# Sparse attention with a gated FFN on one core: batch 0 takes its near keys from the turned keys and its V products in column halves, ScalarE joins in scaling P, and the order of the instructions is new

## The chip, the core and the metric

The kernel runs on one core of a Trainium2 chip. A core has TensorE (PE, matrix products, with its weight loads listed as PEld), VectorE (DVE), ScalarE (ACT), GpSimd (POOL) and SyncE (SP, which issues DMAs). Each engine works through its own list in order; semaphores hold an instruction until its inputs are there and its output's place is free. The metric is the device time of one execution in microseconds (us), as the median of several runs.

## What is computed

Block-sparse attention of 4 batches, 8 heads, 768 rows and head size 64, and behind it a gated feed-forward network (FFN). A row may look at its own and the two neighbouring blocks of 32 rows, at the first and the last block, and at three sampled blocks per block of queries; the first and the last block of queries look at all keys.

```python
scores = q @ k.T / sqrt(64)              # per batch and head
mask = near | first or last block (query or key) | sampled blocks
attn = softmax(where(mask, scores, -1e9))
x = (attn @ v)                           # to (3072, 512)
out = (sigmoid(x @ w_gate) * (x @ w_val)) @ w_out   # d_ff = 1536
```

## The kernel before

A small planner class holds some 1,400 operations (`P(name, engine or engines, estimated duration, function, ...)`). The durations take no part when the kernel is built: `Planner.run` (L207) reads the table `ORDER` (L51 to L172) and issues the operations in that order. An item is `name:engine` and the numbers of the buffers or banks that it takes; engines are P, A (ACT), D (DVE), G (POOL) and S (SP). `+n` on a PE item puts n filler matmuls of 128x512 on zeros ahead of it (L1064), so PE is never idle long.

Each batch goes through these operations (batch number first, then the block or step):

- `ldk`, `ldq`, `ldv` (L415) load and cast to f16, issued by POOL. For batches 1 to 3 `rrk`, `rrq` put rows in order on POOL (L529). `trk`, `trq` turn K and Q on PE (L549 in batch 0, L545 later), `evk`, `evq` bring them from PSUM to the tiles KT and QT (L565 to L569) on ACT or DVE.
- `vsh` copies V by rows (L578, on DVE), `scr` writes it to a scratch tensor in DRAM (L586, L590, by SP). From there `w` (L662, SP) loads windows of near V rows into V1, and `vg` (L729, SP, three DMAs a block) the sampled V rows into V2. `vfl` (L627) fills the rows of the first and last block into V1 and V2, on POOL, or DVE in batch 0. `regSP` and `regPOOL` load the sampled block numbers into registers.
- Keys: each of 11 steps takes two blocks of queries. `kfl` puts the first and last key block in a tile KG, `kg` gathers the sampled ones there (L698, POOL), and `kw` copies the near keys there too (L712, on POOL or DVE). `sc` is then 16 score matmuls of 256 columns (L768) and 8 or 16 mask matmuls (L757), all on quarter-width tiles of the array (two row halves, four column quarters).
- `mx` takes the row maximum (L780, DVE), `ex` the exponential with the row sum, in two halves (L790, ACT), `rz` the reciprocal (L799, DVE), and `sl` scales P by it: one instruction of 512 elements on POOL (L808) or two of 256 on DVE (L811). `tp` turns P on PE (L823), `te` copies it out of PSUM as PTS (L829, ACT or DVE).
- `pv` is the product with V (L841): per step 16 matmuls with 128 columns of V as weights and 64 columns moving, of which only half of each result is wanted. `xe` copies the wanted halves to XT, one instruction per half of the partitions (L868, L870), on ACT or DVE.
- The first and last block of queries are dense: `dsc` (16 matmuls of 384 columns, L897), `dmx` (L908), `dex` (L914), `dsl` (L923), `dtp` (L931), `dte` (L940), `dpv` (32 matmuls, L951), `dxe` (L975, L977). In batch 0 the keys lie in KT with 8 neighbours together, and `dsc` reads every eighth, so that it writes PSUM without gaps.

The FFN takes the rows in nine groups of 128 to 512. For each of 12 slices, `pg` and `pu` are four matmuls each (L1010), `th` a tanh on ACT (L1019), `h` the product on DVE (L1024); then `py` is 12 matmuls for each 128 rows (L1041), `ys` scales (L1048 DVE, L1050 ACT) and `st` stores (L1055). The weights come in nine loads `wg`, `wv`, `wo` of three parts each (L429, L437), issued by POOL. Groups 0 and 1 hold 128 rows each of batch 0; group 2 has 256 rows and begins when batch 0's attention is nearly done. From there on the FFN of one batch runs between the attention steps of the next.

PSUM has eight banks: scores take pairs of 0, 1, 2 (and 5, 6 for batch 0's first steps), P and V products 3 and 4, the FFN 5, 6 and 7. Three options matter here. `merge` 'm' is the scheme with near keys in KG; '.' puts masks first and takes near keys (96 columns) straight from KT and the others (160) from KG, in two matmuls. `tiled` 'u' is the V product above; 't' takes only the wanted half: weights of 64 columns, 32 columns moving, twice as many matmuls, and one copy instruction instead of two. `sl` names the engines that may scale P.

## Time and profile before

| | |
|---|---|
| median of 3 runs | 338.52 us (337.54 to 338.83) |
| the profiled execution | 338.99 us |
| its span | 337.1 us |
| instructions | 11706 |
| matmuls that are fillers | 113 |
| DMA packets, bytes | 43001, 42.09 MB |
| mean of all DMA queues | 125 GB/s |
| granted PE clock | full in every slice of the span |

The span runs from the first to the last instruction of the profiled execution. In what follows, rows of the profile give the engine, the line of the kernel, the operation, output <- input by the names of the tiles, the partitions and elements and the count. Rows by shape end in busy time in us, the mean of one in ns, and the idle time of the engine ahead of them with what ended it. Timelines and the chain of work that ended last begin with start and length in us. Matmuls overlap, so the cost of one in a row of many is the distance of the starts.

### The profile page before, as it was taken

What the parts mean: (1) busy time and instruction counts of PE and PEld (TensorE: products, weight loads), DVE (VectorE), ACT (ScalarE), POOL (GpSimd) and SP (SyncE); (2) the same over time, 40 slices, a digit from 0 to 9 for tenths busy, and PEclk for the clock granted to TensorE, in tenths of its full rate; (3) what the DMA queues carried; (4) which work ended last, traced back from release to release, by engine and by line L of the source; (5) the groups of instructions that cost most, each with busy time, mean ns of one, the idle gap of its engine ahead of it and who ended that gap; (6) DMA issues with size and microseconds to landing.
All of it is one profiled execution on the core that took longest, in us unless ns stands there. A gap on an engine that the chain in (4) does not pass through costs nothing.

```text
span 337.1 us, 11706 instructions
## 1 busy us (share of the span) xinstructions
PE 320.3 (95%) x4241; PEld 193.6 (57%) x4241; DVE 239.5 (71%) x502; ACT 201.0 (60%) x596; POOL 161.8 (48%) x408
## 2 busy tenths in 40 slices
PE   8999889999898989999999999999999999999995
PEld 3535557758755776787466555555555554554442
DVE  5588987577789997677997978788886774313320
ACT  2439786643676785566676666878965664433311
POOL 7675674835677836256678275656535400000000
PEclk9999999999999999999999999999999999999999
DMA  7997799985961446656995322342033234020012
GB/s 124 206 253 156 164 210 245 216 176 152 176 169 31 124 125 127 156 150 132 209 179 167 103 72 92 83 128 73 24 82 105 81 106 136 12 93 2 0 62 93
DMA packets 43001, 42.09 MB, mean 125 GB/s; under 512 B 6432, under 2 KB 39776, under 8 KB 42848
## 3 DMA queue, kind: packets, MB, share of 16 engines
q1 hardware_dynamic: 28768, 27.19, 27.2%
q0 software_dynamic: 14176, 14.16, 26.8%
q8 instruction: 33, 0.54, 0.6%
q14 instruction: 24, 0.20, 0.2%
HBM read 46.05 MB, written 9.44 MB: 165 GB/s over the span
## 4 chain that ended last, share of the span: by engine, by line
PE 75%; DVE 15%; ACT 4%; issue 3%; POOL 1%; POOLq 0%; DVEq 0%; ACTq 0%
PE pall L1010 31%; PE pall L1041 15%; PE pall L1064 7%; PE pall L823 5%; PE pall L841 5%; DVE NM L780 4%; PE pall L768 4%; DVE P L811 2%; ACT P L790 2%; DVE HT L1024 2%; PE pall L951 2%; PE pall L545 2%; PE pall L897 2%; PE pall L931 2%; DVE PTS L829 1%
## 5 line engine op out<-in xcount | busy, mean ns | idle before, releaser
L790 ACT ACTIVATE P<-pall,NM 128x256 f16<-128x256 f32 x176 | 81.4, 475 | 25.2 <-DVE NM L780 21.4
L1024 DVE SCALAR_TENSOR_TENSOR HT<-TH,pall 128x512 f16<-128x512 f32 (+2 forms) x108 | 53.6, 504 | 36.5 <-PE pall L1010 22.4
L1019 ACT ACTIVATE TH<-pall 128x512 f32<-128x512 f32 (+2 forms) x108 | 48.6, 458 | 48.6 <-PE pall L1010 41.4
L808 POOL TENSOR_TENSOR P<-P,ZZ 128x512 f16<-128x512 f16 x46 | 47.4, 1042 | 41.2 <-DVE ZZ L799 30.3
L1041 PE MATMUL pall<-wo,HT 128*128 128x512 f16 x288 | 65.5, 379 | 0.6 <-DVE HT L1024 0.6
L780 DVE TENSOR_REDUCE NM<-pall 128x4 f32<-128x1024 f32 x44 | 53.6, 1220 | 12.8 <-PE pall L757 8.6
L1010 PE MATMUL pall<-XT,wv 128*128 128x256 f16 (+2 forms) x336 | 55.5, 287 | 3.5 <-DVE HT L1024 2.5
L1010 PE MATMUL pall<-XT,wg 128*128 128x256 f16 (+2 forms) x336 | 55.6, 288 | 1.0 <-ACT TH L1019 0.8
L698 POOL COPY KG<-KT 128x64 f32 x264 | 53.0, 251 | 4.2 <-PE pall L757 2.2
L1010 PEld LDWEIGHTS <-wv 128*128 128x128 f16 x432 | 37.9, 98 | 26.7 <-issue 6.4
L1010 PEld LDWEIGHTS <-wg 128*128 128x128 f16 x432 | 37.6, 98 | 24.9 <-issue 3.9
L1041 PEld LDWEIGHTS <-HT 128*128 128x128 f16 x288 | 27.1, 98 | 32.5 <-issue 1.9
L790 ACT ACTIVATION_READ_ACCUMULATOR P<-pall,NM 128x1 f32 x176 | 36.3, 206 | 0.0
L1064 PE MATMUL pall<-WZ 128*128 128x512 f16 x113 | 30.8, 409 | 1.2 <-DVE WZ L369 1.2
L712 POOL COPY KG<-KT 128x384 f32<-128x384 f32 (+1 forms) x25 | 12.4, 497 | 37.8 <-PE pall L757 17.9
L811 DVE TENSOR_SCALAR P<-P,ZZ 128x256 f16<-128x256 f16 x84 | 28.4, 388 | 0.7
L823 PE MATMUL pall<-ident,P 128*128 128x128 f16 x352 | 26.4, 219 | 1.7 <-DVE XT L868 0.9
L823 PEld LDWEIGHTS <-P 128*128 128x128 f16 x352 | 21.3, 98 | 6.9 <-issue 3.9
L1010 PE MATMUL pall<-XL,wv 128*128 128x512 f16 x96 | 23.8, 379 | 0.0
L1010 PE MATMUL pall<-XL,wg 128*128 128x512 f16 x96 | 23.5, 379 | 0.0
L829 ACT COPY PTS<-pall 128x1024 f16<-128x1024 f16 x17 | 17.2, 1013 | 6.8 <-PE pall L823 6.7
L829 DVE COPY PTS<-pall 128x1024 f16<-128x1024 f16 x27 | 18.3, 680 | 3.3 <-PE pall L823 3.2
(103 smaller groups left out, 438.6 us busy)
## 6 DMA issues: line engine op xcount, KB each, us to landing
out_dram<-YS SPq DMA_DIRECT2D x24, 256.0 KB, 2.2
stg<-in_q_dram POOLq DMA_DIRECT2D x4, 768.0 KB, 10.7
stg<-in_v_dram POOLq DMA_DIRECT2D x4, 768.0 KB, 9.1
V2C<-scr SPq DMA_DIRECT2D x96, 32.0 KB, 1.8
V2D<-scr SPq DMA_DIRECT2D x78, 32.0 KB, 2.1
stg<-in_k_dram POOLq DMA_DIRECT2D x3, 768.0 KB, 9.7
scr<-stg SPq DMA_DIRECT2D x12, 192.0 KB
V1C<-scr SPq DMA_DIRECT2D x5, 384.0 KB, 4.1
```

The lines of the kernel that those rows point to most:

```text
L698: pin(nc.gpsimd.tensor_copy(t[:, :, u, KO[r] + (2 + n) * BLK : KO[r] + (3 + n) * BLK].bitcast(f32), KT[r].bitcast(f32)[:, :, bass.ds(regs[ ...
L780: pin(nc.vector.tensor_reduce(NM[o.slots[hz][1]][:, 0:4].rearrange("p (h u) -> p h u", h=2), t, axis=AX.X, op=ALU.max, negate=True))
L790: pin(nc.scalar.activation(pb[:, hh, u, :], t[:, hh, u * 256 : u * 256 + 256], AF.Exp, bias=NM[z][:, 2 * hh + u : 2 * hh + u + 1], scale=1 ...
L808: pin(nc.gpsimd.tensor_tensor(pb, pb, z[:, 2 * hh : 2 * hh + 2].unsqueeze(2).broadcast_to([128, 2, 256]), op=ALU.mult))
L811: pin(nc.vector.tensor_scalar(pb[:, u, :], in0=pb[:, u, :], scalar1=z[:, 2 * hh + u : 2 * hh + u + 1], scalar2=None, op0=ALU.mult))
L823: pin(nc.tensor.transpose(t[:, m * 128 : m * 128 + 128], pb[:, hh, u, c * 128 : c * 128 + 128], ident))
L829: pin(copy(o)(PTS[pl.handles[hTS][1]].rearrange("p m n -> p (m n)"), banks[pl.handles[hT][1]].bitcast(f16)))
L1010: pin(nc.tensor.matmul(t, wt[:, c, f_ * 128 : f_ * 128 + 128], XT[g][:, c, :], start=(c == 0), stop=(c == 3)))
L1019: pin(nc.scalar.activation(TH[o.slots[ht][1]][:, 0:n], banks[pl.handles[hg][1]][:, 0:n], AF.Tanh, bias=0.0, scale=0.5))
L1024: pin(nc.vector.scalar_tensor_tensor(HT[:, f_, hoff : hoff + n], in0=TH[pl.handles[ht][1]][:, 0:n], scalar=1.0, in1=banks[pl.handles[hv][1 ...
L1041: pin(nc.tensor.matmul(t, HT[:, f_, hoff + tt * 128 : hoff + tt * 128 + 128], wo[:, f_, :], start=(f_ == 0), stop=(f_ == NF - 1)))
L1064: pin(nc.tensor.matmul(banks[7], WZ[:, 0:128], WZ, start=True, stop=True))
```

## The change

1. **Near keys of batch 0.** `merge` goes from 'mmmm' to '.mmm': the 11 copies `kw0` are gone, and each score step of batch 0 has 32 matmuls (16 of 96 columns, 16 of 160) for 16.
2. **V products of batch 0.** `tiled` goes from 'uuuu' to 'tuuu': 32 matmuls a step for 16, 64 for 32 in the dense ones, and one `xe` or `dxe` copy for two.
3. **Dense scores of batch 0** read KT with four neighbours in a run and write them 96 elements apart in PSUM.
4. **ACT may scale P** (two activations of 256 with a scale per row) and copy near keys. Over all batches POOL scales 31 halves for 46, DVE 31 for 42, ACT 26 for none. ACT copies near keys four times.
5. **Other engines and queues.** `vsh0` moves from DVE to POOL; three of the six window loads of batch 0 go from SP's queue to POOL's; the fills of batches 2 and 3 become two DMAs by SP each. `te` is on DVE 32 times for 27.
6. **A new order**, with 109 fillers for 113. Ahead of batch 0's first dense score stand 47 for 44, from there to the first FFN matmul 48 for 60, behind it 14 for 9. Three weight loads are issued ahead of the mask's constants. Six score steps for seven and two P transposes for four come before the first FFN matmul. From the first matmul of group 2 on, PE's list holds the same operations, but for three V products of batch 0 in the new form.

```diff
- 'sl': ['PD', 'PD', 'PD', 'PD'],
+ 'sl': ['PDA', 'PDA', 'PDA', 'PDA'],
- 'tiled': 'uuuu',
+ 'tiled': 'tuuu',
- 'merge': 'mmmm'}
+ 'merge': '.mmm'}
...
+    def queue(o):
+        return {"SP": nc.sync, "ACT": nc.scalar, "POOL": nc.gpsimd}[o.eng]
...
         def f_vsh(o):
+            if o.eng == "POOL":
+                pin(nc.gpsimd.tensor_copy(by_row(V0.bitcast(f32), D // 2), by_head(stg[pl.handles[hv][1]].bitcast(f32), D // 2).rearrange("p h j d -> p j h d")))
+                return
...
             def f_fl(o, x=x):
+                if o.eng == "SP":
+                    for vt, ps, t0 in ((V1, slice(96, 128), 0), (V2, slice(0, BLK), S - BLK)):
+                        src = scr[b][t0 : t0 + BLK, :]
+                        pin(nc.sync.dma_start(vt[x][ps], bass.AP(tensor=src.tensor, offset=src.offset, ap=[[DM, BLK], [0, VW], [1, DM]])))
+                    return
...
-                    pin(nc.sync.dma_start(V1[x][0:96, s0 : s0 + n, :], src))
+                    pin(queue(o).dma_start(V1[x][0:96, s0 : s0 + n, :], src))
...
                 def f_kw(o, st=st, hkg=hkg):
+                    if o.eng == "ACT":
+                        c = nc.scalar.copy
...
             def f_sl
                     for u in range(2):
+                        if o.eng == "ACT":
+                            pin(nc.scalar.activation(pb[:, u, :], pb[:, u, :], AF.Copy, scale=z[:, 2 * hh + u : 2 * hh + u + 1]))
+                            continue
...
             def f_dsc
-                            ks = ks.rearrange("d (p j) -> d j p", j=TJ) if b == 0 else ...
+                            ks = ks.rearrange("d (p j) -> d p j", j=TJ)[:, :, 4 * a : 4 * a + 4] if b == 0 else ...
-                            dst = dst.rearrange("q (j p) -> q j p", p=TP) if b == 0 else ...
+                            dst = dst.rearrange("q (j p) -> q p j", p=TP) if b == 0 else ...
```

The new table up to the first FFN matmuls (the old one's beginning is `wz:D cdma:S ldk00:G2 gv0:S ldk01:G ldq00:G1 memset:G idx:D ldv00:G3 mask:D`):

```diff
+wz:D cdma:S ldk00:G3 gv0:S ldk01:G ldq00:G2 ldv00:G1 wg0:G wv0:G wg1:G memset:G mask:D trk000:P1+23 trk001:P2
+evk001:A trk002:P0+4 evk000:D trk003:P2 evk003:A idx:D evk002:D regPOOL0_0:G kfl01:G trq001:P3+13 kfl00:G trq002:P0
+evq001:A trq000:P2 kg0_6:G1 evq002:A evq000:D trq003:P3+1 kg0_4:G0 gc0:A evq003:D dsc0_0:P12+6 dmx0_00:D6 vsh0:G0
+dmx0_01:D7 dex0_00:A0 dex0_01:A1 kfl02:G sc0_6:P0+9 scr0:S vfl0C:G mx0_6:D3 sc0_4:P3+1 regSP0_0:S mx0_4:D5 ex0_60:A0
+kg0_8:G2 dsl0_00:D ex0_40:A1 kg0_10:G0 dtp0_00:P00+9 ex0_41:A regPOOL0_1:G dte0_00:A rz0_4:D sc0_8:P3+4 dsl0_01:D
+mx0_8:D1 ex0_61:A dtp0_01:P1+1 rz0_6:D sl0_40:D sl0_61:A vfl0B:D sl0_41:A w0_4:G0 vg0_5:S dte0_01:A tp0_4:P01+8
+kg0_12:G1 ex0_80:A1 vg0_7:S kg0_14:G2 sc0_12:P2+4 ex0_81:A dpv0_0:P1 mx0_12:D4 vg0_6:S sc0_10:P3 te0_4:D ex0_120:A2
+dxe0_0:D vg0_4:S kg0_16:G0 mx0_10:D2 sl0_60:A ex0_121:A tp0_6:P02+7 wv1:G w0_8:S0 te0_6:D ex0_100:A0 wg2:G vg0_9:S
+sc0_14:P1+1 mx0_14:D0 kg0_18:G1 ex0_101:A pv0_4:P1+2 pv0_6:P0 vg0_10:S xe0_4:A regPOOL0_2:G rz0_8:D sl0_80:D xe0_6:A
+rz0_10:D sl0_101:D sl0_100:A pg0_0:P00+2 vfl0D:D pu0_0:P1 vg0_8:S th0_0:A2 tp0_10:P12 wv2:G ex0_140:A0 h0_0:D
...
```

259 lines of the change are left out of this document (126 added, 133 removed).

## The prediction, made before the changed kernel was run

> **What bounds the kernel now.** I read the page's busy line first, then its chain by engine, then the busy time by stage. The first two:
>
> ```profile
> PE 320.3 (95%) x4241; PEld 193.6 (57%) x4241; DVE 239.5 (71%) x502; ACT 201.0 (60%) x596; POOL 161.8 (48%) x408
> ...
> PE 75%; DVE 15%; ACT 4%; issue 3%; POOL 1%; POOLq 0%; DVEq 0%; ACTq 0%
> ```
>
> TensorE (PE) is busy for 320.3 of 337.1 us and makes up 75% of the chain that ends last; VectorE (DVE) makes up 15%. ScalarE (ACT) and GpSimd (POOL) hardly appear. So what counts is what PE has to do, and how long it stands still. The stages are cut at the first dense score of batch 0 (17.04), the first FFN matmul (41.88) and the first matmul of FFN group 2 (79.38); the columns are stretch, its length, busy time (and instructions) of PE, weight loads, DVE, ACT and POOL, granted clock, DMA share, GB/s.
>
> ```profile
> 0.00:17.04 17.04, 15.84 (x174) 7.57 (x174) 8.92 (x22) 6.33 (x8) 12.32 (x36) 1.00 1.00 165
> 17.04:41.88 24.84, 23.72 (x357) 12.04 (x358) 22.01 (x45) 16.70 (x57) 16.21 (x45) 1.00 0.88 191
> 41.88:79.38 37.50, 33.71 (x565) 24.36 (x563) 27.99 (x67) 21.80 (x78) 22.74 (x40) 1.00 1.05 204
> 79.38:110.00 30.62, 28.12 (x440) 20.99 (x438) 25.47 (x58) 19.88 (x68) 20.89 (x66) 1.00 0.63 131
> 110.00:200.00 90.00, 86.32 (x1327) 59.19 (x1326) 75.43 (x151) 60.18 (x175) 51.70 (x112) 1.00 0.60 141
> 200.00:333.50 133.50, 132.59 (x1396) 69.46 (x1392) 79.66 (x163) 75.56 (x211) 37.94 (x113) 1.00 0.24 74
> ```
>
> After 200 us PE stands for 0.9 us in all; between 79.38 and 333.5 for 2.5 + 3.7 + 0.9 = 7.1. An order can hardly take more than that there. The front looks as full, but 113 of its matmuls are fillers (L1064, written `+n` in the order), and busy time includes the tail that a matmul runs over the next one. So I count PE's front from one start to the next:
>
> ```profile
> 14.58 1.48 PE pall L549 x64
> ...
> 18.56 3.99 PE pall L1064 x18
> ...
> 33.76 1.09 PE pall L951 x32
> ...
> 60.07 0.47 PE pall L841 x16
> ...
> 67.87 5.29 PE pall L1041 x24
> ```
>
> From the chain in order of time (start, us): 64 turning matmuls 1.48, or 23.1 ns each; a filler 3.99/18 = 0.222; a dense V product 1.09; a V product of one step 0.47 (16 at 29 ns); two output products 5.3.
>
> ```profile
> 41.88 0.39 PE L1010 MATMUL pall<-XT,wg 128*128 128x128 f16 x4
> 42.10 0.39 PE L1010 MATMUL pall<-XT,wv 128*128 128x128 f16 x4
> ...
> 43.74 0.41 PE L768 MATMUL pall<-KG,QT 64*32 64x256 f16 x16 [0.19 <-ACT P L790]
> 43.97 0.27 PE L757 MATMUL pall<-mrow,ones 64*32 64x192 bf16 x8
> 44.17 0.62 PE L823 MATMUL pall<-ident,P 128*128 128x128 f16 x8
> 44.63 0.39 PE L1010 MATMUL pall<-XT,wg 128*128 128x128 f16 x4
> ...
> 79.38 0.60 PE L1010 MATMUL pall<-XT,wg 128*128 128x256 f16 x4
> ```
>
> From the PE timeline: an FFN product of group 0 takes 42.10 - 41.88 = 0.22; the 16 score matmuls of a step take 0.23 (14.4 ns each) and its 8 mask matmuls 0.20 (25 ns each), a score step thus 0.43; the eight transposes of a step 0.46.
>
> With these, and the counts of the ORDER table, PE's work from 17.04 to 41.88 is: dense score 1.5, 60 fillers 13.3, 7 score steps 3.0, 6 transposes of P (two of them dense) 2.8, dense V 1.1, two V products 0.9: 22.6 of 24.8, so 2.2 idle. From 41.88 to 79.38: 48 FFN products 10.7, 4 score steps 1.7, 8 transposes 3.7, 6 V products 2.8, dense score 1.5, outputs 5.3, 3 turnings 1.1, dense V 1.1, 9 fillers 2.0: 29.9 of 37.5, so 7.6 idle. **The front thus has 9.8 us of real idle time, the rest 7.1.**
>
> What makes the idle time is mostly DVE. One case:
>
> ```profile
> 47.76 3.29 POOL L698 COPY KG<-KT 128x64 f32 x18
> ...
> 47.80 2.10 DVE L811 TENSOR_SCALAR P<-P,ZZ 128x256 f16<-128x256 f16 x2
> ...
> 51.05 0.38 PE L1010 MATMUL pall<-XT,wv 128*128 128x128 f16 x4 [1.64 <-DVE HT L1024]
> ```
>
> Two scalings of P on DVE take 2.10 us while POOL copies sampled keys at the same time; the FFN evacuation queued behind them is late, and PE waits 1.64.
>
> **The change, part by part.** First PE.
>
> 1. Near keys unmerged in batch 0: each of 11 steps has 32 matmuls of 96 and 160 columns for 16 of 256; the columns are the same. If columns set the pace it costs nothing, at the mask's 25 ns it costs 0.80 - 0.23 = 0.57 a step. The same tile form goes at 14.4 ns in the trace, so I take 32 x 14.4 - 230 = 0.23 a step: **+2.5** (0 to +6.3).
>
> The Trainium skill ("TensorE: Matmul & The Clock Gate", section "Wait — 56ns, not 53.3ns?") says that starts of matmuls never come closer than about 25 ns. The 14.4 ns of L768 contradict it for quarter-width tiles; the mask's 25 ns would fit. By that rule this part would cost 6.3.
>
> 2. V products in column halves: 32 matmuls of 32 columns for 16 of 64. The only half-width rows are the turnings at 23.1 ns: 0.74 for 0.47, +0.27 in each of 11 steps; dense 64 x 23.1 = 1.48 for 1.09, twice: **+3.0 and +0.8** (at 14.4 ns nothing, at 25 ns +3.6 and +1.0).
>
> 3. Dense scores of batch 0: keys now read four in a row instead of one in eight, but written to PSUM with a step of 96 elements.
>
> ```profile
> 17.04 1.53 PE L897 MATMUL pall<-KT,QT 64*32 64x384 f16 x16
> ...
> 122.63 0.82 PE L897 MATMUL pall<-KT,QT 64*32 64x384 f16 x16
> ...
> 163.11 0.53 PE L897 MATMUL pall<-KT,QT 64*32 64x384 f16 x16
> ```
>
> Batch 0 takes 1.53 with keys one by one; later batches read four in a row and take 0.82 and 0.53, writing without a step. The read side is nearest to these; for the unseen write side I take the slower one: 0.71 saved, twice: **-1.4** (0 to -2.0).
>
> Here the Trainium skill speaks against the change: "SBUF — State Buffer", section "Door 1: The DMA port swizzle (why `[64,N]` ≈ `[32,N]`)", gives SBUF lines of 16 bytes, with which the 1.53 against 0.53 agrees, but PSUM lines of 8 bytes and says that a non-contiguous PSUM pattern slows matmuls much. No row here shows a matmul that writes with a step. By that rule the 1.4 would stay away.
>
> 4. Fillers: 109 for 113, **-0.9**; three more before the first dense score, twelve fewer from there to the FFN, five more behind.
>
> Three V products and no score come after the start of group 2 (+0.8); from there on the lists of PE hold the same work. So PE has 2.5 + 3.8 - 1.4 - 0.9 = 4.0 more to do, 3.2 of it before group 2.
>
> Then the other engines, from the rows by shape:
>
> ```profile
> L808 POOL TENSOR_TENSOR P<-P,ZZ 128x512 f16<-128x512 f16 x46 | 47.4, 1042 | 41.2 <-DVE ZZ L799 30.3 <-PE pall L1010 4.6 <-PE pall L757 3.6
> L811 DVE TENSOR_SCALAR P<-P,ZZ 128x256 f16<-128x256 f16 x84 | 28.4, 388 | 0.7
> L1019 ACT ACTIVATE TH<-pall 128x256 f32<-128x256 f32 x36 | 13.8, 386 | 10.7 <-PE pall L1010 7.6 <-DVE HT L1024 1.8 <-ACT XT L977 0.5
> ...
> L829 DVE COPY PTS<-pall 128x1024 f16<-128x1024 f16 x27 | 18.3, 680 | 3.3 <-PE pall L823 3.2
> L829 ACT COPY PTS<-pall 128x1024 f16<-128x1024 f16 x17 | 17.2, 1013 | 6.8 <-PE pall L823 6.7
> ...
> L712 DVE COPY KG<-KT 128x768 f16<-128x768 f16 x17 | 7.9, 466 | 0.0
> ...
> L565 ACT COPY KT<-pall 128x768 f16<-128x768 f16 x6 | 4.7, 803 | 4.1 <-PE pall L549 2.6 <-PE pall L545 1.5
> ...
> L868 DVE CAST XT<-pall 64x256 f16<-64x256 f32 x10 | 4.2, 420 | 0.4 <-PE pall L841 0.3
> L868 ACT CAST XT<-pall 64x256 f16<-64x256 f32 x10 | 3.6, 363 | 0.8 <-PE pall L841 0.7
> ...
> L529 POOL COPY stg<-stg 96x2048 f32<-96x2048 f32 x6 | 11.4, 1897 | 11.9 <-DVE stg L578 6.7 <-DMA V2D<-scr 4.3 <-PE pall L951 0.8
> ...
> L578 DVE COPY XL<-stg 96x4096 f16<-96x4096 f16 x1 | 1.2, 1208 | 0.0
> ```
>
> 5. Scaling P: POOL 46 pieces to 31 at 1.04, DVE 42 to 31 at 2 x 0.388, ACT 0 to 26. ACT's price isn't in the trace: its 256-wide tanh takes 0.386, so 2 x 0.39 = 0.77 (bounds: L868's 0.363 for as many elements, L565's 0.803 for three times as many). POOL -15.6, DVE -8.5, ACT +20. Behind a scaling on ACT stand exps, which free the score banks that the next score step needs; ACT is busy 16.7 of 24.8 us and 21.8 of 37.5 in the front, so I count no wait.
>
> 6. DVE in batch 0: 6 near copies away (6 x 0.466), 3 scalings (2.3), the copy of V (1.2), and XT copies of 2 x 0.42 on six steps become one of 0.42 on three (-3.8); two more PTS copies (+1.4). Together **-8.7 of the 50.0** that it works from 17 to 79 us. ACT there: 7 scalings +5.4, two PTS copies fewer -2.0, XT copies 5 x 0.73 to 8 x 0.36 -0.7, one KT copy -0.8: +1.9 of 38.5.
>
> 7. Near-key copies on ACT, four in batches 1 to 3 at some 0.80 (L565): +3.2 in 230 us with PE busy beside it; cost 0. Fills of V windows in batches 2 and 3 go from POOL (2 x 1024 elements, some 1.9 by L529's 2048) to two SyncE (SP) DMAs; behind them stand only SP's window loads and gathers, for which I see no wait of PE in the waits view; cost 0, at worst an estimated 1.
>
> 8. The V copy and window loads on POOL. Their rows:
>
> ```profile
> 20.19 0.34 SPq L586 DMA_DIRECT2D scr<-XL  x1
> 26.51 0.33 SPq L662 DMA_DIRECT2D V1C<-scr  x1
> ...
> 25.63 1.25 POOL L698 COPY KG<-KT 128x64 f32 x6 [1.05 <-issue]
> ```
>
> V's write to scratch starts at 20.19 and lands by 26.51 (6.3 us). DVE's copy of 1.2 ended at that start, so it began at 19.0; POOL's takes 1.9 (L529 again). Begun no later, the write starts by 20.9 and lands by 27.2. POOL reaches its first window load after a fill (1.9), two gathers (1.25 each) and a register load (1.05, the wait in the last row), at 26.4: it waits 0.8 at most. Behind it stand the gathers of step 12, whose score PE reaches near 30. Cost 0; if the write lands 3 us later still, those 3. Moving the mask behind three weight loads holds one KT copy behind it on DVE, and is done well before the first score near 21.
>
> **The sum.** Dense score at 17.04 + 3 x 0.222 = 17.7; work to the FFN 0.8 + 48 fillers 10.7 + 6 scores 4.0 + 4 transposes 1.8 + dense V 1.5 + two V 1.5 = 20.3; from there to group 2 10.7 + 3.3 + 4.6 + 4.4 + 0.8 + 5.3 + 1.1 + 1.5 + fillers 3.1 = 34.8: group 2 at 72.8 plus idle, before 69.6 plus 9.8. No row says how much idle time goes; the bounds are nothing and all. I take half, since DVE loses a sixth of its work there and POOL the copies that it collides with: 72.8 + 4.9 = 77.7 for 79.4, **-1.7**. Behind: +0.8, and of 7.1 idle I let 2.5 go (batches 1 and 3 lose 12 scalings on DVE, batch 2 gains 4): -1.7. Sum -3.4 on the profiled execution's 338.99 (span 337.1 and 1.9 around it): 335.6. That execution is 0.5 above the median of 338.52, so I say **335.1**.
>
> **The rivals.** About 0.5%, 1.7 us, can be told from no change here.
>
> - *PE pays in full, idle stays* (slower). PE's 4.0 more are certain in kind, the relief isn't: fillers already cover where PE would wait, and a filler isn't shortened by an earlier input. With no idle gone: 338.5 + 4.0 = 342.5. It is slower than 0.5% while less than 2.3 of 16.9 us idle goes. For it: PE's 95%; against it: DVE's 2.10 us above.
> - *ACT takes DVE's place* (slower). In batch 0 exps wait behind scalings, the front's idle stays (+4.9) and ACT's net 1.9 is added: 341.9. For it: ACT's share of 67% in the first stage; against it: 4% of the chain.
> - *Short matmuls at the mask's pace.* All at 25 ns: 3.8 more for scores, 0.8 more for V: 339.7, no change. L768 speaks against it. The Trainium skill's rule of part 1 would have it so.
> - *The dense scores don't gain*: the step of the writes eats what the reads save, 335.1 + 1.4 = 336.5, still faster; the forecast's range holds it (0.15 of its 0.45). No row decides. The Trainium skill's rule of part 3 would have it so.
> - *An even trade*: the moves are real, but the relief equals what PE pays: 338.5.
>
> **Chances.** Forecast (331 to 336.8) 0.45; better, with V at 14.4 ns or more idle gone, 0.08; no change (even trade 0.15, 25 ns 0.07) 0.22; PE in full 0.15; ACT 0.10. So faster 0.53, within 0.5% 0.22, slower 0.25. The range 330 to 343 leaves out what lies beyond the best and the worst, some 0.15.
>
> **What would show it.** Step 1: the score matmuls of batch 0 at 14 ns or at 25; step 2: a V product at 0.47 or 0.74; step 3: the dense score at 0.5 to 0.8 or at 1.5; the first FFN matmul near 39 and group 2 near 78; ACT's scaling at 0.39 a piece; PE idle after group 2 below 5. I am wrong if group 2 starts after 80, if ACT's exps become what score matmuls wait for, or if PE's idle time behind 80 us grows.

## The result, and the profile after

The changed kernel took 342.36 us (median of 4 runs, 341.35 to 343.16) beside 338.44 for the kernel before: a ratio of 1.0115, 95% interval 1.0077 to 1.0152. It is slower, where I had forecast 335.1. Timed a second time it stood at 1.0068 (1.0035 to 1.0101; a_again below). Ratios, here and below, are taken over executions in the faster of two states alone, medians over all; three of the twelve of the second timing were in the slower one. The profiled execution has a span of 341.4 us and took 343.16.

The page's busy line, its chain by engine and the chain by line (line numbers from here on are those of the kernel after; its run is meant by "after"):

```profile
PE 323.2 (95%) x4653; PEld 200.6 (59%) x4653; DVE 219.7 (64%) x458; ACT 223.0 (65%) x653; POOL 138.0 (40%) x381
...
PE 65%; DMA 9%; DVE 8%; SPq 5%; issue 4%; ACT 3%; POOL 3%; POOLq 0%; DVEq 0%; ACTq 0%
PE pall L1029 30%; PE pall L1060 16%; PE pall L842 4%; DMA V1D<-scr 4%; SPq L745 4%; PE pall L860 4%; PE pall L784 3%; DMA scr<-XL 2%; PE pall L551 2%; DMA V2A<-scr 2%; DVE HT L1043 2%; PE pall L970 1%; PE pall L865 1%; PE pall L950 1%; DVE NM L796 1%
```

PE is as busy as before (95%), and DVE's share of the chain fell from 15% to 8%, as the change wants. But DMA stands there with 9% and SP's queue with 5%, which were not in the chain before: V's write to scratch and the loads and gathers of V windows (`V1D<-scr`, `V2A<-scr`, L745). The stages again, cut at the same three events (columns as in the prediction):

```profile
17.47:42.14 24.67, 20.76 (x466) 11.75 (x466) 17.52 (x29) 16.71 (x57) 18.08 (x53) 0.96 0.84 174
42.14:84.17 42.03, 38.97 (x816) 30.26 (x815) 25.32 (x63) 26.13 (x93) 19.76 (x31) 0.94 0.99 191
84.17:110.00 25.83, 25.48 (x444) 18.85 (x446) 17.13 (x39) 20.78 (x66) 18.80 (x55) 1.00 0.72 153
110.00:200.00 90.00, 86.34 (x1315) 60.15 (x1315) 71.84 (x148) 73.42 (x210) 38.41 (x102) 1.00 0.61 145
```

The first dense score starts at 17.47 (before 17.04), the first FFN product at 42.14 (41.88), group 2 at 84.17 (79.38). From there to the end it is 341.4 - 84.17 = 257.2, before 337.1 - 79.38 = 257.7. So **the whole loss, 4.8 us, lies ahead of group 2**, nearly all of it between the first FFN product and group 2: 42.03 for 37.50. And the granted clock, 1.00 in every row of before, is 0.96 and 0.94 in the two front rows.

The PE timeline of after shows where:

```profile
35.98 0.21 PE L865 MATMUL pall<-PTS,V1C 128*64 128x32 f16 x2
39.80 0.21 PE L865 MATMUL pall<-PTS,V2C 128*64 128x32 f16 x2 [3.62 <-DMA V2C<-scr]
...
42.14 0.63 PE L1029 MATMUL pall<-XT,wg 128*128 128x128 f16 x4
42.56 0.63 PE L1029 MATMUL pall<-XT,wv 128*128 128x128 f16 x4
...
59.79 0.21 PE L865 MATMUL pall<-PTS,V2A 128*64 128x32 f16 x2 [1.52 <-DMA V2A<-scr]
...
60.93 0.63 PE L1029 MATMUL pall<-XT,wv 128*128 128x128 f16 x4
61.36 0.63 PE L1029 MATMUL pall<-XT,wg 128*128 128x128 f16 x4
```

The first V product issues its two products on the window (V1C) at 35.98 and then stands 3.62 us for the gathered rows (V2C). The FFN products behind it start 0.42 apart, where 0.22 is their pace at full clock. The same again at 59.79: 1.52 us for V2A, and the half clock up to 64. In the kernel before the same V product starts later and stands for nothing:

```profile
36.07 2.55 PE L1064 MATMUL pall<-WZ 128*128 128x512 f16 x11
38.61 0.41 PE L768 MATMUL pall<-KG,QT 64*32 64x256 f16 x16
...
39.04 0.20 PE L841 MATMUL pall<-PTS,V1C 128*128 128x64 f16 x1
39.08 0.19 PE L841 MATMUL pall<-PTS,V2C 128*128 128x64 f16 x1
```

Eleven fillers and the score step of blocks 16 and 17 lie where after stands; the rows have come by 39.04. The way of the rows is on SP's queue (start, length of the issue, number of transfers). First after, then the row of before that answers to its second:

```profile
19.36 0.34 SPq L595 DMA_DIRECT2D scr<-XL  x1
27.00 7.97 SPq L745 DMA_DIRECT2D V2C<-scr  x12
35.03 0.41 SPq L676 DMA_DIRECT2D V1D<-scr  x1
35.63 11.22 SPq L745 DMA_DIRECT2D V2D<-scr  x12
```

```profile
27.04 7.36 SPq L729 DMA_DIRECT2D V2C<-scr  x12
```

V is written to scratch from 19.36 and has landed at 27.0; then twelve gathers of 32 rows are issued at some 0.66 us each, to 35.0, and by the wait's end the last lands shortly before 39.8. In before the issues start at 27.04. So the rows leave at the same time in both; but the new order sends for blocks 5, 7, 6, 4 (before: 6, 5, 4, and 7 later), so the rows of block 4, which the first V product needs, are the last of the twelve (no run sends them first). **In after the V rows set the first FFN product**; its PE is there 3 us sooner than PE in before. POOL meets the same write:

```profile
27.27 0.72 POOL L676 DMA_DIRECT2D V1C<-scr  x1 [3.03 <-DMA scr<-XL]
...
33.70 0.76 POOL L431 DMA_DIRECT2D wv<-in_moe_w_val_dram  x1
34.45 0.75 POOL L431 DMA_DIRECT2D wg<-in_moe_w_gate_dram  x1
```

It stands 3.03 us at its first window load, and the second chunk of wv and the third of wg, queued behind that, go out only at 33.7 and 34.5, into the stretch of the gathers.

Last the prices of PE, from the starts of neighbouring rows of after, and the row of before that follows its dense score of 17.04:

```profile
25.48 0.28 PE L773 MATMUL pall<-mrow,ones 64*32 64x192 bf16 x8
...
25.98 0.39 PE L1083 MATMUL pall<-WZ 128*128 128x512 f16 x1
...
30.80 1.19 PE L975 MATMUL pall<-DPT,XL 96*64 96x32 f16 x64
31.92 0.28 PE L773 MATMUL pall<-mrow,ones 64*32 64x192 bf16 x8
...
68.41 0.21 PE L865 MATMUL pall<-PTS,V1A 128*64 128x32 f16 x2
...
69.03 0.33 PE L773 MATMUL pall<-mrow,ones 64*32 64x160 bf16 x16
...
72.11 0.84 PE L916 MATMUL pall<-KT,QT 64*32 64x384 f16 x16
72.88 5.35 PE L1060 MATMUL pall<-wo,HT 128*128 128x512 f16 x24
```

```profile
18.50 4.06 PE L1064 MATMUL pall<-WZ 128*128 128x512 f16 x18
```

A score step of batch 0 takes 25.98 - 25.48 = 0.50 (before 0.43), a V product 0.62 (0.47), a dense V product 1.12 (1.09), a dense score 72.88 - 72.11 = 0.77 (before 18.50 - 17.04 = 1.46).

### The profile page after: what moved, and what is told of

It reads as the page before. It is cut to its first block, busy times and chain, and to the rows that moved or that the text cites. A ratio compares the mean times of both kernels' runs of the same rounds, so it can differ in the third digit from the quotient of the medians.

```text
span 341.4 us, 12502 instructions
## 1 busy us (share of the span) xinstructions
PE 323.2 (95%) x4653; PEld 200.6 (59%) x4653; DVE 219.7 (64%) x458; ACT 223.0 (65%) x653; POOL 138.0 (40%) x381
## 4 chain that ended last, share of the span: by engine, by line
PE 65%; DMA 9%; DVE 8%; SPq 5%; issue 4%; ACT 3%; POOL 3%; POOLq 0%; DVEq 0%; ACTq 0%
PE pall L1029 30%; PE pall L1060 16%; PE pall L842 4%; DMA V1D<-scr 4%; SPq L745 4%; PE pall L860 4%; PE pall L784 3%; DMA scr<-XL 2%; PE pall L551 2%; DMA V2A<-scr 2%; DVE HT L1043 2%; PE pall L970 1%; PE pall L865 1%; PE pall L950 1%; DVE NM L796 1%
## 5 line engine op out<-in xcount | busy, mean ns | idle before, releaser
L1043 DVE SCALAR_TENSOR_TENSOR HT<-TH,pall 128x512 f16<-128x512 f32 (+2 forms) x108 | 53.5, 505 | 40.2 <-PE pall L1029 24.5
L1029 PE MATMUL pall<-XT,wv 128*128 128x256 f16 (+2 forms) x336 | 56.8, 293 | 1.5 <-DVE HT L1043 0.8
L1029 PE MATMUL pall<-XT,wg 128*128 128x256 f16 (+2 forms) x336 | 56.8, 293 | 1.5 <-DVE HT L1043 0.8
L824 POOL TENSOR_TENSOR P<-P,ZZ 128x512 f16<-128x512 f16 x31 | 32.2, 1045 | 59.8 <-DVE ZZ L815 42.1
L1029 PEld LDWEIGHTS <-wg 128*128 128x128 f16 x432 | 38.4, 100 | 26.9 <-issue 5.2
L806 ACT ACTIVATION_READ_ACCUMULATOR P<-pall,NM 128x1 f32 x176 | 36.3, 206 | 0.0
L842 PE MATMUL pall<-ident,P 128*128 128x128 f16 x352 | 27.7, 221 | 2.1 <-DVE P L830 1.4
L842 PEld LDWEIGHTS <-P 128*128 128x128 f16 x352 | 22.6, 99 | 7.7 <-DVE P L830 1.9
L828 ACT ACTIVATE P<-P,ZZ 128x256 f16<-128x256 f16 x52 | 23.4, 507 | 1.4 <-DVE ZZ L815 1.3
L1029 PE MATMUL pall<-XL,wv 128*128 128x512 f16 x96 | 24.2, 379 | 0.0
L848 DVE COPY PTS<-pall 128x1024 f16<-128x1024 f16 x32 | 21.7, 682 | 2.6 <-PE pall L842 2.6
L784 PE MATMUL pall<-KG,QT 64*32 64x256 f16 (+1 forms) x704 | 18.8, 264 | 0.3 <-POOL KG L712 0.2
L1069 ACT ACTIVATE YS<-pall 128x512 f32<-128x512 f32 x17 | 10.1, 596 | 12.5 <-PE pall L1060 12.3
```

What stands on the lines that cost most here:

```text
L784: pin(nc.tensor.matmul(t[32 * p : 32 * p + 32, hh, u * 256 + c0 : u * 256 + c1], QT[r][kp, p, i * BLK : (i + 1) * BLK], src, start=(merged ...
L806: pin(nc.scalar.activation(pb[:, hh, u, :], t[:, hh, u * 256 : u * 256 + 256], AF.Exp, bias=NM[z][:, 2 * hh + u : 2 * hh + u + 1], scale=1 ...
L824: pin(nc.gpsimd.tensor_tensor(pb, pb, z[:, 2 * hh : 2 * hh + 2].unsqueeze(2).broadcast_to([128, 2, 256]), op=ALU.mult))
L828: pin(nc.scalar.activation(pb[:, u, :], pb[:, u, :], AF.Copy, scale=z[:, 2 * hh + u : 2 * hh + u + 1]))
L842: pin(nc.tensor.transpose(t[:, m * 128 : m * 128 + 128], pb[:, hh, u, c * 128 : c * 128 + 128], ident))
L1029: pin(nc.tensor.matmul(t, wt[:, c, f_ * 128 : f_ * 128 + 128], XT[g][:, c, :], start=(c == 0), stop=(c == 3)))
```

## The experiments

Kernels named a_ start from the kernel after, those named b_ from the kernel before. All times are medians in us; the ratio is to the kernel before, run beside it, with its 95% interval. First V product, first FFN product and group 2 are from the profiled execution, counted from its first dense score (which starts at 15.6 to 18.0 us, with the inputs' loads); clock is the mean between FFN and group 2. Executions of one kernel differ in their mean clock, and in time with it (b_half_gather1: 336.1 to 337.1 with 1.00, 339.0 to 340.4 with 0.987 to 0.995), so single medians are good to a us or two.

| run | total | ratio | V product | FFN | group 2 | clock |
|---|---|---|---|---|---|---|
| before | | 1 | 22.0 | 24.8 | 62.3 | 1.00 |
| after | 342.36 | 1.0115 (1.0077 to 1.0152) | 18.5 | 24.7 | 66.7 | 0.94 |
| a_again | 340.83 | 1.0068 (1.0035 to 1.0101) | 18.5 | 24.5 | 65.8 | 0.98 |
| a_gather1 | 339.15 | 1.0029 (0.9998 to 1.0060) | 18.5 | 20.2 | 64.8 | 1.00 |
| b_gather1 | 337.65 | 1.0004 (0.9984 to 1.0024) | 22.0 | 24.0 | 61.4 | 1.00 |
| a_weights | 341.22 | 1.0112 (1.0074 to 1.0151) | 19.1 | 22.3 | 64.4 | 0.96 |
| a_fill | 341.10 | 1.0103 (1.0067 to 1.0139) | 22.0 | 23.7 | 64.1 | 1.00 |
| b_unmerge | 338.24 | 1.0005 (0.9974 to 1.0036) | 22.2 | 24.9 | 63.2 | 1.00 |
| b_half | 341.72 | 1.0129 (1.0072 to 1.0185) | 22.0 | 24.4 | 64.3 | 0.96 |
| b_dsc | 337.47 | 0.9970 (0.9935 to 1.0005) | 21.7 | 24.5 | 61.3 | 1.00 |
| b_three | 341.65 | 1.0105 (1.0067 to 1.0142) | 21.6 | 23.6 | 67.3 | 0.93 |
| b_two | 337.19 | 0.9978 (0.9948 to 1.0009) | 21.5 | 23.6 | 60.5 | 1.00 |
| a_whole | 341.11 | 1.0078 (1.0036 to 1.0120) | 18.4 | 25.2 | 65.0 | 0.99 |
| b_half_gather1 | 339.96 | 1.0022 (0.9992 to 1.0052) | 22.0 | 24.4 | 61.2 | 1.00 |
| b_half_fill | 341.52 | 1.0098 (1.0066 to 1.0129) | 22.0 | 24.4 | 63.6 | 1.00 |
| b_extra | 344.03 | 1.0188 (1.0140 to 1.0236) | 22.6 | 25.3 | 67.3 | 1.00 |
| b_half_late | 344.75 | 1.0239 (1.0189 to 1.0288) | 22.0 | 24.4 | 64.0 | 1.00 |
| a_whole_fill | 341.22 | 1.0084 (1.0052 to 1.0116) | 21.9 | 24.8 | 65.0 | 1.00 |
| a_whole_nofill | 340.69 | 1.0076 (1.0046 to 1.0106) | 21.9 | 24.2 | 63.4 | 1.00 |
| b_two_mend | 338.45 | 1.0016 (0.9990 to 1.0042) | 21.6 | 24.4 | 64.6 | 0.96 |

**First theory: the V rows.** The new order comes to its first V product over 3 us before the rows are there, stands, and loses the clock. The rivals: PE pays for its extra products; ScalarE's scalings come late.

```diff
@@ f_vg, batch 0 (a_gather1, b_gather1)
-                    for n in range(3):
-                        pin(nc.sync.dma_start(V2[x][(1 + n) * BLK : (2 + n) * BLK, ws, :], ...
+                    pin(nc.sync.dma_start(V2[x][BLK : 4 * BLK, ws, :], scr[b][(i - 1) * BLK : (i + 2) * BLK, :]))
```

> The kernel after, with each sampled V gather of batch 0 as one copy of 96 neighbouring rows in place of three copies of 32 rows at the sampled places (same bytes, one issue for three; the sampled V rows of batch 0 are so replaced by others, that part of the computation is changed). Theory 1, the V rows' way gates the early stage (write to scratch, 12 issues of 0.66 us each, landing): PE no longer stands 3.6 us before the first V product nor 1.5 us before that of blocks 12 and 13, the half clock behind each goes too (about 3 us); first FFN product near 37 in place of 42.1, group 2 near 76 in place of 84.3, total 334 to 336. Theory 2, PE pays for batch 0's extra products: the total stays at 342 within 1. Theory 3, ScalarE's scaling is late: the total stays at 342 too.

> The kernel before with the same edit (sampled V rows of batch 0 replaced by neighbouring ones, one copy for three). Theory 1: before has fillers and a score product where after stands idle, and its PE order doesn't change, so it gains less than after does: 335.5 to 338, 0.5 to 3 less than before. Theories 2 and 3: no change within 0.5 per cent (338.4).

The waits for V rows went and the first FFN product came at 37.63, as the theory had it; the total fell by about 3 us beside after's first timing and 1.7 beside its second, not by 7. b_gather1 gained nothing that can be told, so in before the V rows don't set the time. The stretch behind the first FFN product took 44.6 us, longer than in after (42.0), in spite of a clock of 1.00. Its row, and two lines of PE's timeline:

```profile
37.63:82.25 44.62, 37.82 (x815) 27.93 (x814) 28.28 (x67) 26.38 (x93) 23.57 (x39) 1.00 1.00 193
```

```profile
57.66 0.21 PE L864 MATMUL pall<-PTS,V2A 128*64 128x32 f16 x2 [1.81 <-issue]
...
68.33 0.82 PE L915 MATMUL pall<-KT,QT 64*32 64x384 f16 x10
70.59 0.51 PE L915 MATMUL pall<-KT,QT 64*32 64x384 f16 x6 [1.45 <-issue]
```

PE is busy 37.82 us there, 4.1 more than in the row of before (33.71), at full clock. And it stands 1.81 and 1.45 us in the middle of a V product and of a dense score, with nothing that releases it ("issue"). So the V rows are a part of the loss; the theory was short of PE's longer work there and of these two waits.

```diff
@@ ORDER (a_weights)
- w0_4:G0 vg0_5:S ... wv1:G w0_8:S0 te0_6:D ex0_100:A0 wg2:G
+ wv1:G wg2:G w0_4:G0 vg0_5:S ... w0_8:S0 te0_6:D ex0_100:A0
@@ ORDER (a_fill)
- pv0_4:P1+2 ... pv0_12:P0
+ pv0_4:P1+18 ... pv0_12:P0+8
```

> The kernel after with the loads of the second chunk of wv and the third of wg issued by POOL ahead of the first window load, at about 24 us, where POOL stands 3 us for the scratch write, in place of 33.7 and 34.5 us. Theory 1 (the gathers at 27 to 46 us share the DMA engines with these 1 MB): the wait before the first V product falls from 3.6 to 1 to 2 us, that of blocks 12 and 13 goes, total 339 to 341. If the gathers are bound by their issue alone: waits and total stay (342 within 1). Theories 2 and 3: 342 within 1.

> The kernel after with 16 more filler products (0.22 us each, 3.5 us) ahead of the first V product and 8 more (1.8 us) ahead of that of blocks 12 and 13; no work is taken away. Theory 1 with the clock (the wait is the V rows', and the idle PE is then run at half clock for some us): the V products start no later than now, the FFN products behind them take 0.22 us in place of 0.42, total 339.5 to 340.5. If idle time alone counts and the clock follows something else: 342 to 343. Theory 2 (PE work sets the time): 5 us more, 347.

With the weights out of the way the wait for V2C fell from 3.6 to 1.4, and the first FFN product came 2.4 us earlier: the loads did delay the gathers. PE then stood 1.9 us inside the V product of blocks 12 and 13 instead, again released by nothing, and the clock fell with it; the total hardly moved. a_fill took no work away and added 5 us of fillers; still its group 2 starts 2.6 us before that of after, and its span is 339.2 for 341.4:

```profile
41.62:82.03 40.41, 38.83 (x823) 28.64 (x822) 25.43 (x63) 26.25 (x93) 20.87 (x35) 1.00 1.04 206
```

The clock of 1.00 is what it gains: **the half clock behind the two waits costs after some 2 us** (PE's busy time says the same: 20.76 + 38.97 in after, 19.89 + 37.82 for the same work in a_gather1). The timings don't show this gain: a_fill's median, 341.10, is over the 339.5 to 340.5 expected and lies between the two of after (342.36 and 340.83). The rest of the loss stays with the fillers in place of the waits.

**The parts by themselves, in the order of before.** The three edits of batch 0, one at a time and together (`merge` and `kw0_*` away; `tiled` to `'tuuu'`; the two lines of `f_dsc`):

```diff
@@ TUNE
- 'tiled': 'uuuu',            'merge': 'mmmm'
+ 'tiled': 'tuuu',            'merge': '.mmm'
```

> The kernel before, its order kept, with the near keys of batch 0 read where they are turned (the 11 copies kw0 left out, 16 more products a score step). Theory 1 (the new order's V rows, idle PE and clock make the loss, the parts cost next to nothing): PE pays 0.07 us a step (0.8 in all), DVE and POOL lose 5 us of work, total 337 to 339. Theory 2 (the prediction's price, 0.23 us a step): PE +2.5 us, total 339 to 341.

> The kernel before, its order kept, with only the V products of batch 0 in column halves (32 more products a step, one read of the result for two). Theory 1: 0.15 us a step on PE (1.7 in all), of which the first two steps lie in fillers' time, DVE and ScalarE relieved: total 337.5 to 339.5, and PE's stages grow by no idle time. Theory 2 (0.27 us a step and 0.4 a dense product, 3.8 in all): 341 to 342.

> The kernel before with only the new read of the dense scores of batch 0 (keys read in their order, result written with a step). PE's two dense score steps take 0.84 us in place of 1.53. Theory 1: the first stands ahead of the V rows' gate (about 39 us) and so gains nothing, the second 0.7: total 337 to 338, at most 0.3 per cent faster. The prediction's sum: both count, 1.4 us less, 337.

> The kernel before, its order and its engines kept (no scaling on ScalarE, V copy on DVE, window loads on SP), with the three edits of batch 0 together: near keys unmerged, V products in halves, new dense read. Theory 1: first FFN product at 41 to 42, group 2 at 79 to 80.5, total 337 to 339.5, within 0.3 per cent of before; the loss belongs to the new order. Theory 2: PE's sum of the prediction (2.5 + 3.8 - 1.4), 341 to 343, as slow as after.

Unmerging costs nothing that can be told, and the dense read's gain of 0.3% is just not clear of its interval (to 1.0005). **The halves alone lose 4 us, as much as the whole change**, and b_three with them: the theory that the loss belongs to the new order alone fell. The second theory gave b_half's total (341 to 342), but not its reason, since a V product costs 0.15 us more and not 0.27. The row of b_half between the first FFN product and group 2, and its waits:

```profile
41.33:81.26 39.93, 36.67 (x693) 26.72 (x691) 25.09 (x63) 21.52 (x76) 23.37 (x43) 0.96 1.05 207
```

```profile
48.38 0.21 PE L841 MATMUL pall<-PTS,V2D 128*64 128x32 f16 x2 [1.18 <-DMA V2D<-scr]
...
50.52 0.21 PE L841 MATMUL pall<-PTS,V2D 128*64 128x32 f16 x2 [0.53 <-DMA V2D<-scr]
...
92.64 0.20 PE L841 MATMUL pall<-PTS,V1C 128*64 128x32 f16 x1 [1.40 <-issue]
```

Before stood 1.64 us for DVE at 51.05 and 0.85 at 41.43. In b_half those waits are gone, which fits DVE's reading each result once; in their place PE stands 1.18 and 0.53 for the V rows (V2D) and the clock falls to 0.96. And at 92.64 it stands 1.40 inside a V product, released by nothing. b_three has three such waits ahead of group 2, 0.73, 0.87 and 2.01 us, and runs at half clock behind the last:

```profile
62.82 0.21 PE L840 MATMUL pall<-PTS,V1A 128*64 128x32 f16 x2 [2.01 <-issue]
```

**Two suspects in each: order and halves.**

```diff
@@ TUNE (a_whole, from after)
- 'tiled': 'tuuu',
+ 'tiled': 'uuuu',
@@ ORDER (b_half_fill, from before with 'tuuu'; b_half_gather1: with the single copies above)
- pv0_8:P0 ... pv0_10:P1
+ pv0_8:P0+6 ... pv0_10:P1+3
```

> The kernel after, its new order and all else kept, with the V products of batch 0 whole again (128 by 64 products, result read in two pieces). Theory A (the halves make the loss: twice the products, PE short of instructions within them, waits for V rows that the faster reads only uncover): total 336.5 to 339, 3 to 5 less than after. Theory B (the new order makes it, V rows gate the first V product 3 us earlier in PE's order): the 3.6 us wait stays and so does the half clock, total 340.5 to 342.

> The kernel before with the V products of batch 0 in halves and each sampled V gather of batch 0 as one copy of 96 neighbouring rows for three of 32 at the sampled places (the sampled V rows are replaced, same bytes). Theory A1 (halves cost what PE then waits for V rows, with the half clock behind it): no wait for V2D, clock 1.00, group 2 at 77 to 78.5, total 337 to 338.5, within 1 of the kernel before with the single copies (337.65). Theory A2 (halves cost PE's instructions themselves): 340.5 to 342, with waits inside products that nothing releases.

> The kernel before with the V products of batch 0 in halves, and 6 more filler products ahead of the V product of blocks 8 and 9 and 3 more ahead of that of 10 and 11 (2 us of fillers where it waited 1.7 us for V rows). Theory A1 with the clock: no wait over 0.3 there, clock 1.00 in place of 0.96 from first FFN product to group 2, group 2 at 79.5 to 80.5 in place of 81.3, total 339.5 to 341. If the clock falls from the narrow products and not from the wait: clock and total stay (341.7), group 2 after 81.

> The kernel before, its order kept, with the near keys of batch 0 unmerged and the new dense read, V products whole: the change without halves, ScalarE's scaling and order. From the parts by themselves (+0.05 and -0.3 per cent): 336.5 to 338, 0 to 0.5 per cent faster than before. If near keys and dense read only fill the wait for V rows: 337.7, no change.

a_whole keeps its wait, and most of the loss:

```profile
40.06 0.20 PE L856 MATMUL pall<-PTS,V2C 128*128 128x64 f16 x1 [4.00 <-DMA V2C<-scr]
```

So with whole products and halves in the two orders the ratios are 0.998 (b_two) and 1.011 (b_three) in the order of before, 1.008 (a_whole) and 1.012 or 1.007 (after) in the new one. **Each of the two loses about 1% by itself, and both together hardly more.** With the V rows early the halves lose less (1.0022, b_half_gather1; its profiled execution has no wait for V2D and starts group 2 no later than b_gather1, 61.2 for 61.4): most of what they lose in b_half goes with the V rows, which are not there when PE comes sooner. Not all: that execution is one of three at full clock, and the median of the twelve, 339.96, is over the 337 to 338.5 expected; no trace shows where the others lost the clock. b_half_fill bears out the clock: with fillers in those waits it stays 1.00 and group 2 starts 0.7 us earlier. But the total stays: behind group 2 it takes 260.8 us for 258.7, where the wait at 92 has grown and the clock halves from 94.5:

```profile
92.54 0.21 PE L841 MATMUL pall<-PTS,V1C 128*64 128x32 f16 x2 [2.55 <-issue]
```

**What the waits are that nothing releases.** A packet of 16.4 KB on the queue named "instruction" (in a_gather1 0.20 MB in 12 packets up to 90 us) precedes each: at 55.3 and 68.2 us in a_gather1, at 90.2 in b_half_fill, 2.3 to 2.4 us before PE goes on. My theory: PE runs out of instructions, since narrower products take more of them for the same work.

```diff
@@ f_pv, batch 0 (b_extra, from before)
+                    for m in range(32):
+                        pin(nc.tensor.matmul(t[64 * (m % 2) : 64 * (m % 2) + 64, 0, 0, 0:32], WZ[:, 0:64], WZ[:, 0:32], ...
@@ ORDER (b_half_late, from b_half_fill)
- ldv20:G0 ... ldk20:G1 ... kw1_8:G1
+ ldv20:G0 ldk20:G1 kw1_8:G1
```

> The kernel before, V products of batch 0 whole, with 32 extra products of zeros (64 weight columns, 32 moving columns, the size of the halves' products) ahead of each of its 11 score steps' V products: as many instructions more on PE as in the halves, and nothing else. Theory I (PE short of instructions): waits of 0.5 to 2.5 us inside operations that nothing releases, a few us after a packet of the instruction queue, total 339.5 to 342. Theory R (the halves lose by V rows that their shorter reads uncover): no such waits, only the products' own time, 0.15 to 0.3 a step, part of it in DVE's waits: total 338 to 340.

> The kernel before with halves and the fillers of b_half_fill, and the loads of batch 2's V and K issued some 12 us later (POOL, ahead of kw1_8), out of the stretch at 86 to 95 us where PE stood 2.55 us inside the V product of blocks 2 and 3. Theory I with late packets (the instruction packet waits behind other transfers): that wait falls under 0.7 and the clock stays 1.00 there, total 338 to 339.5. If the packet's way does not depend on the load of the DMA engines: the wait stays at 1.4 to 2.6, total 341.5.

b_extra, with whole products and 32 idle ones ahead of them, has them: PE's timeline, then the line of the instruction queue from 59.5 to 59.6 us (packets, MB, share of 16 engines):

```profile
47.17 0.68 PE L834 MATMUL pall<-WZ 128*64 128x32 f16 x32
47.78 0.20 PE L840 MATMUL pall<-PTS,V1D 128*128 128x64 f16 x1
...
60.22 0.36 PE L834 MATMUL pall<-WZ 128*64 128x32 f16 x12
62.02 0.49 PE L834 MATMUL pall<-WZ 128*64 128x32 f16 x20 [1.44 <-issue]
```

```profile
q8 instruction: 1, 0.02, 60.1%
```

Twelve of the 32 products ran, then PE stood 1.44 us and went on 2.4 us after the packet; likewise 0.79 at 68.41 (packet 66.2) and 0.87 at 96.88 (94.6). The extra products also cost 47.78 - 47.17 = 0.61 a step themselves, 6.7 in all, which is more than the halves' 0.15. So its trace shows that such waits come with more instructions, but its total (344.03, over the 339.5 to 342 expected) doesn't tell what the halves lose by them. The place of the waits settles what they are. In the 20 traces of the table, 24 waits of over 0.35 us behind the first dense score have no releaser. They are spread over 14 traces, some with whole products (a_whole, b_two). Counted along PE's own instructions, all 24 stand at place 194 or 195 of a block of 256, whatever PE does there, and end 2.2 to 2.9 us after a packet's start; the two of a_gather1 are 512 instructions apart. The queue carries 36 packets in after and 33 in before, and PE's 2 x 4653 and 2 x 4241 products and weight loads make 36.3 and 33.1 blocks of 256. So PE stands there for its next block. The Trainium skill ("Runtime: NRT & Kernel Launch", section "Instruction fetch mechanics") says that instructions are fetched in blocks of 16 KiB, 256 of them, and that crossing a block is mostly hidden. The block size agrees with 16.4 KB and with the places; hidden it was in the profiled executions of before and after, and not in those 14, with waits of up to 2.55 us.

Of b_half_late half came true. The wait at 92 is gone: its packet started 0.8 us after PE had entered the block before, with the DMA engines at a mean share of 0.35 in the 2 us ahead, where in b_half_fill the same packet started after 4.7 us, at a share of 1.16. But POOL's later loads made PE wait 2.99 us for sampled keys, and the total is the worst of all. The 20 traces say the same of 456 packets between 15 and 200 us: the median start is 0.4 us after PE enters the block before where that share is under 0.5, and 3.2 us where it is over 1.1. So a block comes late where other loads fill the DMA engines; more and shorter products add to it, as b_extra shows.

```profile
112.45 0.28 PE L763 MATMUL pall<-KG,QT 64*32 64x256 f16 x2 [2.99 <-POOL KG L693]
```

**What the new order costs besides.**

```diff
@@ ORDER (a_whole_fill, from a_whole)
- pv0_4:P1+2
+ pv0_4:P1+18
@@ ORDER (a_whole_nofill, from a_whole_fill: every +n between pg0_0 and pg2_0)
- pg0_0:P00+2 pg0_1:P10+3 pg0_2:P10+1 ... pu0_7:P1+3 ...
+ pg0_0:P00 pg0_1:P10 pg0_2:P10 ... pu0_7:P1 ...
```

> The kernel after with whole V products in batch 0 and 16 more fillers ahead of the first V product, where the version without them waited 4.0 us. If wait, half clock and halves make up after's loss: first FFN product at 41 to 42, clock 1.00, total 337.5 to 339.5. If the new order has another cost of its own: over 340.

> The kernel after with whole V products in batch 0, 16 more fillers ahead of the first V product, and none of the 16 fillers that stand between it and the output products of group 1 (0.21 us each, 3.4 us). Theory W (PE's own work behind the first FFN product sets that stretch): group 2 at 78 to 79 in place of 81.7, total 337.5 to 339. Theory D (something else ends last there, the fillers stand in its waits): waits of 2 to 3 us appear in the place of the fillers, group 2 stays at 81 to 82, total 341, or more where the clock falls.

> The kernel after itself, for its time beside the runs of this call: 341.5 to 343 by all theories.

a_whole_fill has 0.51 us of the 4.0 left, no half clock and no halves, and is still at 1.0084: the new order has a cost of its own (1.03 us of it one wait for instructions, at 56.55). Without its 16 fillers group 2 starts 1.7 us earlier, not 3.4, and the total hardly moves. The row of that stretch, and PE's waits in it (us in total, times, longest):

```profile
41.40:80.56 39.16, 34.11 (x672) 26.26 (x672) 26.36 (x65) 27.83 (x98) 20.32 (x32) 1.00 1.03 200
```

```profile
PE pall L1024 <- ACT TH L1033: 1.3, 3, 0.9
PE pall L1024 <- ACT XT L882: 1.1, 1, 1.1
...
PE pall L911 <- ACT P L801: 0.4, 1, 0.4
```

PE's work there without fillers, 34.1, compares with 33.7 - 9 x 0.22 = 31.7 in before: 2.4 us more of steps stand behind the first FFN product, some of which stood ahead of it in before, where fillers now are (the score step of blocks 16 and 17 is one). And 2.8 us of waits for ACT appear, for 0.4 in before; ACT is busy 27.8 us there for 21.8. The fillers lay in these waits. "The new order" means here all that a_whole keeps of the change, ACT's scaling and the moves to POOL's queue too; no run parts these from the order itself.

**A better version?** b_two leaves out the halves and the new order; b_two_mend adds two repairs.

```diff
@@ ORDER (b_two_mend, from b_two)
- pv0_8:P0 ... vfl1D:G ... kg1_8:G
+ pv0_8:P0+4 ... kg1_8:G vfl1D:G
```

> The kernel before with near keys unmerged and the new dense read in batch 0, V products whole, 4 more fillers ahead of the V product of blocks 8 and 9 (a wait of 0.84 there for V rows) and POOL's fill of batch 1's V window D moved behind the sampled keys of blocks 8 and 9 (a wait of 1.94 for them at 101 us). If the waits and the half clock behind them kept the version without from its gain: clock 1.00, total 335.5 to 337, 0.4 to 0.8 per cent faster than before; otherwise 337 to 338.

In b_two group 2 starts 1.8 us earlier than in before, and behind it 337.4 - 77.15 = 260.3 us are left for 257.7: PE stands 1.94 us at 101 for sampled keys and the clock halves. The repair took that wait away (257.6 behind group 2), but with four fillers more the V product of blocks 8 and 9 stood 2.47 us for 0.84, since its rows came later, and the total, 338.45, is over the 335.5 to 337 expected:

```profile
50.89 0.19 PE L835 MATMUL pall<-PTS,V2D 128*128 128x64 f16 x1 [2.47 <-DMA V2D<-scr]
```

b_two (0.9978) and b_dsc (0.9970) are the best that I ran; both intervals touch 1, so no version is shown to beat before.

## Why the prediction was wrong

The failed step is **the sum's idle time, and part 8 under it**. I took half of the front's 9.8 us of idle time away and set the first FFN product at 39, since DVE and POOL lose work. By the prices measured above, PE's work from the dense score to group 2 is 62 fillers and 48 FFN products 24.4, 11 score steps 5.5, 14 transposes 6.4, 8 V products 5.0, dense V 2.2, dense scores 1.5, outputs 5.4, turnings 1.1: 51.5 us (forecast 55.1). What is not work, waits, gaps and half clock, is 66.7 - 51.5 = 15.2 (forecast 4.9, before 9.8). The prices were 3.6 us too high, the idle time 10.3 too low.

- *Part 8*: the write's times were right (start 19.4 for "by 20.9", landed 27.0 for 27.2), "Cost 0" was wrong. I stopped at the landing and did not walk on through twelve gathers at 0.66 us to the first V product. This chain ends at 39.8 in after, and the first FFN product follows at 42.14; a start at 39 was not to be had with V rows that leave no sooner than in before. POOL's wait was 3.0, not 0.8.
- *The sum*: it didn't ask what is late next where a stall goes. DVE's waits went, as forecast, and V rows came in their place: 3.62 and 1.52 in after, 1.18 and 0.53 in b_half. Steps that the new order puts behind the first FFN product I counted as work there, but with a start at 39 that the V rows don't allow.
- *Part 1*: the mechanism was right, the size not: 0.07 a step for 0.23. *Part 2*: 0.15 for 0.27; but the halves cost more than their time, by the V rows and the instruction blocks that PE then waits for, which no step foresaw.
- *Part 3* was right: the dense score went from 1.46 to 0.77, 0.69 saved for 0.71. The Trainium skill's rule on PSUM patterns, which I let speak against it, is not borne out by this write. *Part 4*: the count was right, 14 fillers behind the first FFN product for 9 among it.
- *Part 5*: the price was 0.90 for 0.77 (two pieces, ACT's rows), with no wait seen while fillers cover it; without them PE waits 2.8 us for ACT (a_whole_nofill), though for tanh, X copies and exps, and that the scalings delay these is not shown. *Part 6*: DVE works 42.8 us there, -7.2 for -8.7. *Part 7* held: all waits of over 0.45 us behind group 2 in after are for DVE.
- Behind group 2 the kernel gained 0.5, forecast 1.7.

Of the rivals, "PE pays in full" has the measured time (342.5), but not its reason: PE's products cost less than forecast. Likewise "ACT takes DVE's place": its waits are real but lie under fillers. So the total's agreement with the first is luck. The 25 ns rival fell: 40 products of a score step start in 0.50 us, 32 of a V product in 0.62, 12.5 and 19.4 ns apart.

What stays open: how after's loss divides between the new order and the halves, which don't add up, and within the order between it, ACT's scaling and the queues. The second V wait of after (59.79) is for V rows, at place 146 of its block; in a_again the same V product stands 0.96 us at place 195, for instructions.

## What to carry to other kernels

Before crediting a relieved engine with idle time, walk the other inputs of the first product behind that idle time to their landing, gathers with every issue; the latest of them is the new bound, and an order that comes to it sooner only stands there. Work that an order moves from ahead of such a gate to behind it is paid there, while its old place stands idle or holds fillers. Ask of any edit that splits products how many instructions a us it makes PE take, and what loads run where a block of them ends. Fillers in waits that can't be removed keep the clock, though here no total gained by it.

## What the hardware showed

- A wait can be paid again in the clock: after 3.62 and 1.52 us of standing, FFN products took 0.42 us for 0.22, in the second case until 64.1. In the 20 traces half clock is granted for 3.41 us, or twice that, at a time (but for the last us of an execution). It came within 2 us of the end of each of the six waits of 2.4 us or more, and of 4 of the 14 waits between 1.4 and 2.1 us: a_gather1 stood 1.81 us at 57.66 and kept 1.00. Nor does it need a long wait: b_three had it from 80.6 to 87.4 with none over 0.45 us since 62.82. The Trainium skill ("TensorE: Matmul & The Clock Gate", section "Part 1: The HAM clock gate (the "warmup" mystery)") has the clock set by activity windows of some 3.4 us; the length of 3.41 agrees, and a window that runs freely would explain why equal waits have unequal ends, though no run here shows the window.
- PE can stand inside an operation for want of instructions: 24 waits of 0.38 to 2.55 us, each at place 194 or 195 of a block of 256 instructions and ended 2.2 to 2.9 us after the start of a 16.4 KB packet on the instruction queue. The packet starts late where the DMA engines are full (median 3.2 us against 0.4).
- Products of 32 columns on half of the array's columns start 19.4 ns apart in a V product of batch 0 (32 in 0.62 us) and 17.5 ns in a dense one (64 in 1.12); the 32 products of b_extra, on zeros, took 19 ns each.
- Matmuls that write PSUM with a step of 96 elements and read keys four in a row took 0.77 us for 16 of 384 columns, where 1.46 was taken by writes in a row and reads of every eighth key.
